# A fused attention, mixture and MLP kernel: MLP weights written to scratch as two parts, and adjoining turns summed in one set of banks

## The chip, the cores and the metric

The kernel runs on one core of a Trainium2 chip. The time is device microseconds for one execution. Before the change three runs gave 1144.51, 1145.59 and 1153.5 us; the median is 1145.59 us.

## What is computed

Three layers follow one another on 1152 tokens of 512 features. The first is attention, local and coarse; its output is the token matrix x. The other two are these, cut to what the change touches:

```python
def _moe_ref(x, w_gate, w1, w2):
    P = ...                      # 8 rounds of row and column scaling of exp(x @ w_gate)
    for e in range(8):           # w1[e] 512 x 1024, w2[e] 1024 x 512
        out += P[:, e:e + 1] * (np.maximum(x @ w1[e], 0.0) @ w2[e])
    return out

def _moe2_ref(x, w_in, w_out):   # w_in 512 x 2048, w_out 2048 x 512
    h = x @ w_in
    g = np.maximum(h, 0.0) + np.log1p(np.exp(-np.abs(h)))
    return g @ w_out
```

w_in and w_out arrive as 64-bit floats; the kernel makes 32-bit floats of them on the chip.

## The kernel before

**Two parts of every operand.** A matmul here takes 32-bit operands in a rounded form. Every operand is therefore split in two: `hi`, the value cast to the rounded form, and `lo`, the value minus `hi`. Three matmuls (hi by hi, hi by lo, lo by hi) make one product.

**Turns.** The MLP is treated as two more experts (`e` = 8 and 9) beside the eight of the mixture. The tokens are in two sets: `s` = 0 with four tiles of 128 tokens (256 columns in each half) and `s` = 1 with five (320 columns in each half). The hidden units of an expert are in four pieces `p`, and `g` is a pair of pieces. A turn is one (e, g, s, p), 80 in all, in the list `steps`. `first(n)` makes the hidden units of a turn by seven products of a fast 2x2 scheme (line 578, banks `m`), so that w1 is kept as OPS = 7 blocks, the first four of them sums. Between the products ACT copies (`t1`, `t5`, `u2`, line 587) and DVE adds (`c`, line 592). `hidden` then applies the activation: for the mixture one ACT and one DVE instruction (lines 539 and 540), for the MLP nine on ACT, DVE and POOL in a chain (lines 545 to 556). `second(n)` multiplies by w2 into banks `yps` (line 637), one for each token tile.

**Banks and sums.** Before the change two turns (`p` even and `p` odd) are summed in the banks. Then `weigh` (lines 648 to 656) reads each bank: into `acc` by a copy the first time, by a plain add for experts 0, 8 and 9 (line 650), and with the gate's weight for experts 1 to 7 (line 654).

**Order of the turns.** Experts 1 to 6 take the sets in the order 0, 1, 0, 1. Experts 0 (its second half), 7, 8 and 9 take them so that several turns of one set follow one another:

```python
late = [(0, 1), (1, 1), (1, 0), (0, 0)]
turn = {E - 1: late, E: late, NE - 1: [(0, 0), (0, 1), (1, 1), (1, 0)]}
```

**Weights.** `fetch_first` and `fetch_second` load the weights of a piece into a place of three (`wp`, three buffers each of w1h, w1l, w2h, w2l). They are called when PE's last use of the place three fetches ago has been issued. For the mixture the raw weights come to a `raw` tile (two buffers), ACT casts hi, POOL and DVE subtract. For the MLP the same is done from scratch in HBM: w1 by two loads of 448 KB (line 117), two casts (line 118), and for each a subtraction on POOL of 512 columns and one on DVE of 384 (line 120); w2 by one load (line 147), two casts (line 151) and two subtractions on POOL (line 152). The MLP does ten such fetches of w1 and ten of w2.

**Conversion.** From turn 12 to turn 58, `convert` (lines 159 to 199) makes 32 pieces of MLP weights, two in three turns: it loads 64-bit values into a `raw` tile, makes 32-bit floats in `cva` with seven DVE instructions (lines 177 to 187), and for w_in (the first 16 pieces) also the four sums on POOL (line 106). It writes `s_in` in three stores and `s_out` in one. `cva` and `sums` share two buffers (`smp`) with the sums that `fetch_first` makes for the mixture.

**What sets the order.** PE's instructions stand in the order written. Those of DVE, ACT, POOL and SP are put in order by a scheduler when the kernel is built, and each engine then runs its own list in that order, waiting where it must. All DMAs are issued by SP.

## Time and profile before

| what | value |
|---|---|
| median of three runs | 1145.59 us |
| the profiled execution's own time | 1142.73 us |
| its span, first to last instruction | 1140.6 us |
| mean granted TensorE clock | 0.981 of full speed |
| PE busy | 1069.6 us (94%) |
| DVE busy | 818.9 us (72%) |
| ACT busy | 532.2 us (47%) |
| POOL busy | 497.6 us (44%) |
| moved by DMA | 93.74 MB, mean 82 GB/s |

Attention fills about the first 150 us, with the first turns of expert 0 beside it. Experts 1 to 7 follow, and the MLP runs from about 910 us to the end. PE is the engine with the most work. A reader looks for the stretches in which it stands idle, and for the engine that ended each idle time.

### The profile page before, as it was taken

Reading aid. Unit: us, or ns where it says so; the run is one execution under the profiler, and the core shown is the slowest. Engines: PE = TensorE matmul, PEld = TensorE weight load, DVE = VectorE, ACT = ScalarE, POOL = GpSimd, SP = SyncE. Lnnn points to the kernel's source line nnn. Section 1 sums busy time; section 2 is a strip of 40 time slices with the busy share of each in tenths; the row PEclk is TensorE's granted clock in tenths of the full one; section 3 lists DMA queues with packets and bytes.
Section 4 is the critical chain, followed back from the end, with each engine's and each line's share of the span. In section 5 each row is a group of like instructions: output and inputs, shape, how many; then the busy total and the mean of one; then the engine's idle time right before and its main releaser. Section 6 shows DMA issues by size and latency. Waiting matters only on the chain.

```text
span 1140.6 us, 17866 instructions
## 1 busy us (share of the span) xinstructions
PE 1069.6 (94%) x6385; PEld 936.7 (82%) x6385; DVE 818.9 (72%) x1680; ACT 532.2 (47%) x1403; POOL 497.6 (44%) x529
## 2 busy tenths in 40 slices
PE   6799998999999999999999999999999879989998
PEld 5678877888988888888988889888888767877887
DVE  6999756754757677676767666677665788888885
ACT  4677644433324334233333334334423577776773
POOL 6744325373344434443542523424532555465331
PEclk9689999999999999999999999999999989999999
DMA  8554101211232332333222322223231332132002
GB/s 172 127 111 109 50 1 56 72 41 38 91 106 75 122 96 83 97 100 107 72 91 93 111 93 66 83 93 93 87 107 62 102 102 70 33 90 77 25 1 83
DMA packets 107736, 93.74 MB, mean 82 GB/s; under 512 B 34560, under 2 KB 86016, under 8 KB 107648
## 3 DMA queue, kind: packets, MB, share of 16 engines
q1 hardware_dynamic: 107648, 92.61, 27.5%
q8 instruction: 50, 0.82, 0.3%
q14 instruction: 38, 0.31, 0.1%
HBM read 78.69 MB, written 13.89 MB: 81 GB/s over the span
## 4 chain that ended last, share of the span: by engine, by line
PE 49%; DVE 29%; DMA 6%; POOL 5%; ACT 5%; issue 5%; SPq 1%; DVEq 0%; POOLq 0%; ACTq 0%
PE yps L637 22%; PE m L578 22%; DVE c L592 3%; DMA raw<-in_moe_w_in 2%; DVE acc L654 2%; DMA raw<-in_moe_w_out 2%; DVE cva L177 2%; DVE cva L178 2%; DVE xl L224 2%; POOL w1l L141 2%; POOL sums L106 2%; DVE raw L184 1%; DVE cva L181 1%; POOL w2l L152 1%; PE sc L349 1%
## 5 line engine op out<-in xcount | busy, mean ns | idle before, releaser
L578 PE MATMUL m<-xh,w1h 128*128 128x320 f32 (+1 forms) x1120 | 339.7, 303 | 43.0 <-DVE c L592 24.8
L578 PE MATMUL m<-xl,w1h 128*128 128x320 f32 (+1 forms) x1120 | 332.8, 297 | 0.0
L578 PE MATMUL m<-xh,w1l 128*128 128x320 f32 (+1 forms) x1120 | 332.7, 297 | 0.0
L578 PEld LDWEIGHTS m<-xh,w1h 128*128 128x128 f32 x1120 | 212.6, 190 | 76.6 <-DVE c L592 40.8
L578 PEld LDWEIGHTS m<-xl,w1h 128*128 128x128 f32 x1120 | 212.8, 190 | 11.5 <-DVE xl L224 0.3
L578 PEld LDWEIGHTS m<-xh,w1l 128*128 128x128 f32 x1120 | 212.7, 190 | 0.0
L637 PE MATMUL yps<-w2h,hh 128*128 128x512 f32 x520 | 207.5, 399 | 1.7 <-ACT hh L555 1.4
L637 PE MATMUL yps<-w2l,hh 128*128 128x512 f32 x520 | 206.4, 397 | 0.0
L152 POOL TENSOR_TENSOR w2l<-raw,w2h 128x512 fp32r<-128x512 f32 x92 | 125.5, 1384 | 182.6 <-ACT w2h L151 182.5
L637 PE MATMUL yps<-w2h,hl 128*128 128x512 f32 x520 | 204.4, 393 | 0.4 <-DVE hl L556 0.4
L539 ACT ACTIVATE hh<-c 128x256 fp32r<-128x256 f32 (+1 forms) x138 | 60.6, 444 | 213.6 <-DVE c L592 213.6
L141 POOL TENSOR_TENSOR w1l<-sums,w1h 128x512 fp32r<-128x512 f32 x72 | 94.9, 1335 | 131.0 <-ACT w1h L140 93.2
L637 PE MATMUL yps<-w2h,h 128*128 128x512 f32 x400 | 140.7, 392 | 0.0
L654 DVE SCALAR_TENSOR_TENSOR acc<-yps,pr,acc 128x512 f32<-128x512 f32 x126 | 93.7, 744 | 50.4 <-PE yps L637 47.7
L637 PEld LDWEIGHTS yps<-w2h,hl 128*128 128x128 f32 x520 | 98.5, 189 | 23.9 <-DVE hl L556 0.8
L592 DVE TENSOR_TENSOR c<-m,t 128x256 f32<-128x256 f32 (+1 forms) x160 | 72.1, 451 | 58.3 <-PE m L578 57.6
L637 PEld LDWEIGHTS yps<-w2h,hh 128*128 128x128 f32 x520 | 99.1, 191 | 15.8 <-ACT hh L555 1.8
L637 PEld LDWEIGHTS yps<-w2l,hh 128*128 128x128 f32 x520 | 99.1, 191 | 11.7
L540 DVE SCALAR_TENSOR_TENSOR hl<-c,hh 128x256 fp32r<-128x256 f32 (+1 forms) x138 | 74.4, 541 | 33.4 <-ACT hh L539 31.2
L552 POOL TENSOR_TENSOR ab<-ab,up 128x320 f32<-128x320 f32 (+1 forms) x64 | 55.3, 865 | 90.1 <-ACT ln L548 43.1
L637 PEld LDWEIGHTS yps<-w2h,h 128*128 128x128 f32 x400 | 75.4, 188 | 13.4
L106 POOL TENSOR_TENSOR sums<-raw 128x256 f32<-128x256 f32 x72 | 62.1, 883 | 50.0 <-DMA raw<-in_moe_w 38.9
(135 smaller groups left out, 1681.3 us busy)
## 6 DMA issues: line engine op xcount, KB each, us to landing
raw<-in_moe_w SPq DMA_DIRECT2D x72, 256.0 KB
raw<-in_moe_w SPq DMA_DIRECT2D x36, 512.0 KB
raw<-s_in SPq DMA_DIRECT2D x20, 448.0 KB
raw<-in_moe_w_in SPq DMA_DIRECT2D x32, 256.0 KB
raw<-in_moe_w_out SPq DMA_DIRECT2D x16, 512.0 KB
raw<-s_out SPq DMA_DIRECT2D x10, 512.0 KB
s_in<-sums SPq DMA_DIRECT2D x16, 256.0 KB
s_out<-cva SPq DMA_DIRECT2D x16, 256.0 KB
```

Of the source, the lines that this page charges most:

```text
L106: nc.gpsimd.tensor_tensor(sums[i], a, b, op=op)
L141: nc.gpsimd.tensor_tensor(lo[:, part], sums, hi[:, part].bitcast(F32), op=ALU.subtract)
L152: nc.gpsimd.tensor_tensor(lo[:, i], raw[:, i], hi[:, i].bitcast(F32), op=ALU.subtract)
L177: nc.vector.tensor_scalar(a, high, 0x07FFFFFF, 3, op0=ALU.bitwise_and, op1=ALU.logical_shift_left)
L178: nc.vector.scalar_tensor_tensor(out=a, in0=low, scalar=29, in1=a, op0=ALU.logical_shift_right, op1=ALU.bitwise_or)
L539: nc.scalar.activation(hh, c, AF.Relu)
L540: nc.vector.scalar_tensor_tensor(out=hl, in0=c, scalar=0.0, in1=hh.bitcast(F32), op0=ALU.max, op1=ALU.subtract)
L552: nc.gpsimd.tensor_tensor(ab, ab, up, op=ALU.subtract)
L578: nc.tensor.matmul(b[:, :h], x[:, i, kk, :], y[s][:, i, kk, :], start=(not more and n == 0), stop=(n == 5), skip_group_check=more,)
L592: nc.vector.tensor_tensor(c, b[:, :h], t, op=ALU.add)
L637: nc.tensor.matmul(y, a[:, f, tok], b[:, f, :], start=(start and m == 0), stop=(stop and m == 5))
L654: nc.vector.scalar_tensor_tensor(out=acc[t], in0=y, scalar=pr[:, t, e : e + 1], in1=acc[t], op0=ALU.mult, op1=ALU.add,)
```

## The change

Scratch now holds both parts of every MLP weight, in the layout of the operand places. `convert` makes them: after the conversion ACT casts hi into the `raw` tile, whose values are no longer needed, and POOL subtracts in place. That is two casts and two subtractions of 128x512 for each w_in piece and one of each for a w_out piece, 48 and 48 in all. A w_in piece is then written by six stores instead of three, in runs of 512 bytes, and a w_out piece by two instead of one. For the MLP `fetch_first` and `fetch_second` only issue two loads each, straight into hi and lo; 896 KB each for w1 and 512 KB each for w2. The casts and subtractions that they had (20 casts of 896 columns, 20 of 512, 40 subtractions on POOL, 20 on DVE) are gone.

A list `begins` marks the turns at which a new sum starts in the banks: where the set changes, or the expert (8 and 9 counting as one), and at the first five. Turns that follow one another in the same set and expert are summed in the same banks. `weigh` is called at the end of a sum, 32 instructions fewer: five plain adds in expert 0, nine weighted ones in expert 7, eighteen plain adds in the MLP.

```diff
-    s_in = scratch("s_in", [F2 // (2 * P), 2, P, OPS, P])
-    s_out = scratch("s_out", [F2, DM])
+    s_in = scratch("s_in", [F2 // (2 * P), 2, P, OPS, 2, P])
+    s_out = scratch("s_out", [F2 // (2 * P), 2, P, 2, DM])
...
         if e >= E:
-            for kk in range(2):
-                raw = rawp.tile([P, OPS, P], F32, tag="raw", name="raw7")
-                nc.sync.dma_start(raw, s_in[n - E * NP, kk])
-                nc.scalar.copy(hi[:, :, kk], raw)
-                for engine, part in zip((nc.gpsimd, nc.vector), parts):
-                    engine.tensor_tensor(
-                        lo[:, part, kk], raw[:, part], hi[:, part, kk].bitcast(F32), op=ALU.subtract
-                    )
+            for i, x in enumerate((hi, lo)):
+                nc.sync.dma_start(x.bitcast(F32), s_in[n - E * NP, i])
             return
...
     def fetch_second(f, n):
...
+        if e >= E:
+            for i, x in enumerate((hi, lo)):
+                nc.sync.dma_start(x.bitcast(F32), s_out[n - E * NP, i])
+            return
...
     def convert(i):
...
+        def parts(x, hi, engine):
+
+            nc.scalar.copy(hi, x)
+            engine.tensor_tensor(x.bitcast(F32R), x, hi.bitcast(F32), op=ALU.subtract)
+
+
+        first = raw.rearrange("p d f c -> p (d f c)").bitcast(F32R)
         if i >= HALVES:
-            nc.sync.dma_start(s_out[rows, :], a)
+            e, h, p = (i - HALVES) // (2 * NP), (i - HALVES) // NP % 2, (i - HALVES) % NP
+            first = first[:, :DM]
+            parts(a, first, nc.gpsimd)
+            for j, x in enumerate((first.bitcast(F32), a)):
+                nc.sync.dma_start(s_out[e * NP + p, j, :, h], x)
             return
         a = a.rearrange("p (q c) -> p q c", q=4)
+        first = first.rearrange("p (q c) -> p q c", c=P)
         sums = smp.tile([P, SUMS, P], F32, tag="sums", name="sums")
         weight_sums([sums[:, i] for i in range(SUMS)], lambda fh, d: a[:, 2 * d + fh])
-        nc.sync.dma_start(s_in[m, kk, :, :SUMS], sums)
-        nc.sync.dma_start(s_in[m, kk, :, SUMS], a[:, 0])
-        nc.sync.dma_start(s_in[m, kk, :, SUMS + 1 :], a[:, 2:4])
+        parts(sums, first[:, :SUMS], nc.gpsimd)
+        parts(a, first[:, SUMS:], nc.gpsimd)
+        for j, x, y in ((0, *[first.bitcast(F32)[:, part] for part in (slice(SUMS), slice(SUMS, 2 * SUMS))]), (1, sums, a)):
+            nc.sync.dma_start(s_in[m, j, :, :SUMS, kk], x)
+            nc.sync.dma_start(s_in[m, j, :, SUMS, kk], y[:, 0])
+            nc.sync.dma_start(s_in[m, j, :, SUMS + 1 :, kk], y[:, 2:4])
...
+    begins = [
+        n == 0 or s != steps[n - 1][2] or min(e, E) != min(steps[n - 1][0], E) or n < BESIDE + 1
+        for n, (e, g, s, p) in enumerate(steps)
+    ]
+    stops = begins[1:] + [True]
...
     def weigh(e, s, i, y):
-        t = TILES[s][i]
+        t, e = TILES[s][i], min(e, E)
...
-        elif e == 0 or e >= E:
+        elif e in (0, E):
...
-                second(n, *hs, i, ys[i], p % 2 == 0, p % 2 == 1)
-                if p % 2:
+                second(n, *hs, i, ys[i], begins[n], stops[n])
+                if stops[n]:
                     weigh(e, s, i, ys[i])
```

PE's list is the same instruction for instruction; the other four lists move. Three places follow, a pair of pieces of before and after each.

ACT's list in the MLP, where the hidden units of turn 72 are begun (`t` and `u` are the copies out of the banks, `ab`, `ln` and `h` belong to the activation, `w2h` to the weights). Before:

```order
1002 L587 COPY t_10935<-m_10928 128x256
1003 L587 COPY t_10944<-m_10937 128x256
1004 L151 CAST w2h<-raw_10914 128x512 x2
1005 L545 ACTIVATE ab<-c_10959 128x256
1006 L555 CAST h_10761<-ab 128x256 x2
1007 L546 ACTIVATE ab<-ab 128x256
1008 L548 ACTIVATE ln<-ab 128x256
1009 L587 COPY u_10979<-m_10928 128x256
```

And in the changed kernel:

```order
1024 L605 COPY t_10945<-m_10938 128x256
1025 L573 CAST h_10795<-ab 128x256
1026 L605 COPY t_10954<-m_10947 128x256
1027 L573 CAST h_10795<-ab 128x256
1028 L563 ACTIVATE ab<-c_10969 128x256
1029 L564 ACTIVATE ab<-ab 128x256
1030 L566 ACTIVATE ln<-ab 128x256
1031 L605 COPY u_10989<-m_10938 128x256
```

The two casts of w2h, which waited for a load from scratch, no longer stand ahead of `u`.

DVE's list at the second piece of w_in that is converted (`cva` and the 64-bit `raw` are the conversion, `c` and `hl` the hidden units). Before:

```order
530 L540 SCALAR_TENSOR_TENSOR h_3529<-m_3530,h_3528 128x320
531 L654 SCALAR_TENSOR_TENSOR acc<-yps,pr,acc 128x512
532 L177 TENSOR_SCALAR cva<-raw_3642 128x512
533 L592 TENSOR_TENSOR c_3699<-m_3692,t_3675 128x256
534 L178 SCALAR_TENSOR_TENSOR cva<-raw_3642,cva 128x512
535 L181 SCALAR_TENSOR_TENSOR cva<-raw_3642,cva 128x512
```

And in the changed kernel:

```order
526 L558 SCALAR_TENSOR_TENSOR h_3526<-m_3527,h_3525 128x320
527 L610 TENSOR_TENSOR c_3703<-m_3696,t_3679 128x256
528 L558 SCALAR_TENSOR_TENSOR hl<-c_3703,hh 128x256
529 L173 TENSOR_SCALAR cva<-raw_3639 128x512
530 L174 SCALAR_TENSOR_TENSOR cva<-raw_3639,cva 128x512
531 L610 TENSOR_TENSOR c_3727<-m_3681,u_3713 128x256
```

The start of the conversion (line 177 before, 173 now) has moved behind the first `c` and `hl` of the next turn.

SP's list at a w_in piece in the middle of the conversion (`raw<-in_moe_w_in` loads the next piece's 64-bit values, `raw<-in_moe_w` weights of the mixture). Before:

```order
97 L198 DMA s_in<-cva 128x128
98 L199 DMA s_in<-cva 128x256
99 L126 DMA raw_4502<-in_moe_w 128x4x128 x2
100 L126 DMA raw_4616<-in_moe_w 128x4x128 x2
101 L197 DMA s_in<-sums 128x512
102 L168 DMA raw_4633<-in_moe_w_in 128x2x256 x2
```

And in the changed kernel:

```order
111 L210 DMA s_in<-raw_4411 128x128
112 L211 DMA s_in<-raw_4411 128x2x128
113 L209 DMA s_in<-raw_4411 128x4x128
114 L210 DMA s_in<-cva 128x128
115 L211 DMA s_in<-cva 128x2x128
116 L209 DMA s_in<-sums 128x4x128
117 L119 DMA raw_4648<-in_moe_w 128x4x128 x2
118 L164 DMA raw_4665<-in_moe_w_in 128x2x256 x2
```

Six stores now stand together, the last three behind POOL's subtractions, and the next loads stand behind all six.

## Rows read from the trace of the kernel before

**Rows 1.** The page: span, then busy time of each engine.

```profile
span 1140.6 us, 17866 instructions
...
PE 1069.6 (94%) x6385; PEld 936.7 (82%) x6385; DVE 818.9 (72%) x1680; ACT 532.2 (47%) x1403; POOL 497.6 (44%) x529
```

**Rows 2.** Stretches: length, PE, PEld, DVE, ACT, POOL busy; clock, DMA share, GB/s.

```profile
270.00:600.00 330.00, 319.67 (x1851) 284.44 (x1849) 226.26 (x392) 114.59 (x268) 143.99 (x172) 1.00 0.30 92
600.00:850.00 250.00, 244.83 (x1396) 217.05 (x1397) 168.65 (x306) 89.93 (x207) 92.88 (x86) 1.00 0.28 91
...
870.00:1075.00 205.00, 180.11 (x1027) 156.34 (x1026) 170.29 (x333) 144.11 (x350) 104.14 (x88) 0.97 0.23 72
```

**Rows 3.** All waits of PE from 270 to 850 us: total, times, longest.

```profile
PE m L578 <- DVE c L592: 15.5, 22, 1.6
```

**Rows 4.** Longest waits of PE from 870 to 1075 us.

```profile
PE m L578 <- ACT u L587: 11.9, 8, 4.7
PE m L578 <- DVE c L592: 8.3, 10, 2.0
PE tp L664 <- ACT xf L667: 1.5, 2, 0.7
```

**Rows 5.** Groups by line, 870 to 1075 us: busy, mean ns, idle before, releasers.

```profile
L120 POOL TENSOR_TENSOR w1l<-raw,w1h 128x512 fp32r<-128x512 f32 x20 | 32.2, 1630 | 27.1 <-ACT w1h L118 27.0
L152 POOL TENSOR_TENSOR w2l<-raw,w2h 128x512 fp32r<-128x512 f32 x20 | 29.8, 1512 | 16.6 <-ACT w2h L151 16.5
L120 DVE TENSOR_TENSOR w1l<-raw,w1h 128x384 fp32r<-128x384 f32 x20 | 19.7, 990 | 4.0 <-ACT w1h L118 4.0
L118 ACT CAST w1h<-raw 128x896 fp32r<-128x896 f32 x20 | 18.0, 942 | 2.3 <-PE m L578 1.4 <-DMA raw<-s_in 0.6
L151 ACT CAST w2h<-raw 128x512 fp32r<-128x512 f32 x20 | 11.4, 617 | 9.4 <-DMA raw<-s_out 8.6 <-PE yps L637 0.4 <-DMA raw<-in_moe_w 0.4
L650 DVE TENSOR_TENSOR acc<-yps,acc 128x512 f32<-128x512 f32 x12 | 8.2, 680 | 0.5 <-PE yps L637 0.5
...
L654 DVE SCALAR_TENSOR_TENSOR acc<-yps,pr,acc 128x512 f32<-128x512 f32 x9 | 6.7, 741 | 1.2 <-PE yps L637 1.2
```

**Rows 6.** Timeline, ACT and PE around two waits: start, length, instruction, idle before.

```profile
929.37 1.15 ACT L151 CAST w2h<-raw 128x512 fp32r<-128x512 f32 x2
936.06 0.64 PE L578 MATMUL m<-xh,w1h 128*128 128x320 f32 x1 [4.74 <-ACT u L587]
1028.19 1.15 ACT L151 CAST w2h<-raw 128x512 fp32r<-128x512 f32 x2 [1.18 <-DMA raw<-s_out]
1031.68 0.35 ACT L587 COPY u<-m 128x256 f32<-128x256 f32 x1
1032.09 0.39 PE L578 MATMUL m<-xh,w1h 128*128 128x256 f32 x1 [2.17 <-ACT u L587]
```

**Rows 7.** One stretch around the longer wait of rows 6, columns as in rows 2.

```profile
926.00:944.00 18.00, 12.35 (x59) 10.73 (x59) 16.77 (x29) 15.14 (x39) 12.01 (x11) 0.72 0.24 81
```

**Rows 8.** Waits of SP's queue over the whole span.

```profile
SPq L117 <- POOL w2l L152: 56.6, 9, 11.3
...
SPq L117 <- DVE w1l L120: 32.6, 5, 18.4
```

**Rows 9.** Groups by line and shape, 270 to 850 us.

```profile
L177 DVE TENSOR_SCALAR cva<-raw 128x512 uint32<-128x512 uint32 x31 | 27.3, 882 | 29.3 <-DMA raw<-in_moe_w_out 11.2 <-DMA raw<-in_moe_w_in 9.9 <-POOL w1l L141 5.6
...
L140 ACT CAST w1h<-sums 128x512 fp32r<-128x512 f32 x48 | 29.5, 615 | 19.7 <-POOL sums L106 19.7
...
L141 POOL TENSOR_TENSOR w1l<-sums,w1h 128x512 fp32r<-128x512 f32 x48 | 63.7, 1344 | 73.2 <-ACT w1h L140 52.5 <-PE yps L637 20.7
```

**Rows 10.** Line 177 over the whole span: ns shortest/median/longest.

```profile
L177 DVE TENSOR_SCALAR cva<-raw x32: 426/430/1506, 295.3 to 856.1; 128x512 uint32<-128x512 uint32 x32
```

**Rows 11.** Timeline, POOL and DVE at one start of a conversion.

```profile
343.81 2.55 POOL L141 TENSOR_TENSOR w1l<-sums,w1h 128x512 fp32r<-128x512 f32 x2 [1.85 <-ACT w1h L140]
345.15 1.50 DVE L177 TENSOR_SCALAR cva<-raw 128x512 uint32<-128x512 uint32 x1 [0.55 <-POOL w1l L141]
```

More of the change, by code (lines that the diff above doesn't have):

```diff
@@ L112, in fetch_first @@
         weights.setdefault(f, {})[0] = hi, lo
-        parts = slice(0, SUMS), slice(SUMS, OPS)
         if e >= E:
-            for kk in range(2):
-                raw = rawp.tile([P, OPS, P], F32, tag="raw", name="raw7")
-                nc.sync.dma_start(raw, s_in[n - E * NP, kk])
-                nc.scalar.copy(hi[:, :, kk], raw)
-                for engine, part in zip((nc.gpsimd, nc.vector), parts):
-                    engine.tensor_tensor(
-                        lo[:, part, kk], raw[:, part], hi[:, part, kk].bitcast(F32), op=ALU.subtract
-                    )
+            for i, x in enumerate((hi, lo)):
+                nc.sync.dma_start(x.bitcast(F32), s_in[n - E * NP, i])
             return
@@ L144, in fetch_second @@
         e, p = divmod(n, NP)
-        w = w2[e] if e < E else s_out[(e - E) * FF : (e - E + 1) * FF, :]
-        raw = rawp.tile([P, 2, DM], F32, tag="raw", name="raw2")
-        nc.sync.dma_start(raw, w.rearrange("(h a p) d -> p h a d", h=2, p=P)[:, :, p, :])
         hi = wp.tile([P, 2, DM], F32R, tag="w2h", name="w2h")
         lo = wp.tile([P, 2, DM], F32R, tag="w2l", name="w2l")
+        weights.setdefault(f, {})[1] = hi, lo
+        if e >= E:
+            for i, x in enumerate((hi, lo)):
+                nc.sync.dma_start(x.bitcast(F32), s_out[n - E * NP, i])
+            return
+        raw = rawp.tile([P, 2, DM], F32, tag="raw", name="raw2")
+        nc.sync.dma_start(raw, w2[e].rearrange("(h a p) d -> p h a d", h=2, p=P)[:, :, p, :])
         for i in range(2):
@@ L152, in fetch_second @@
             nc.gpsimd.tensor_tensor(lo[:, i], raw[:, i], hi[:, i].bitcast(F32), op=ALU.subtract)
-        weights.setdefault(f, {})[1] = hi, lo
     TINY = 2.0 ** -15 * 1.125
@@ L765, in attention_moe_mlp @@
             e, g, s, p = steps[n]
-            if p % 2 == 0:
+            if begins[n]:
                 ys = outputs(s)
```

## The prediction

> **What bounds the kernel now.** I read the page first, then the busy time by stretches, then PE's waits in two of the stretches, then what the change removes and adds there, and last the timeline at single waits. PE is busy for 1069.6 of 1140.6 us [rows 1], so PE bounds the kernel, and a change that leaves its list as it is can win only from the idle time and from TensorE's clock. Where that time lies is shown by the stretches [rows 2]. From 270 to 850 us (experts 1 to 7, with the conversion beside them) PE stands idle for 330 - 319.7 + 250 - 244.8 = 15.5 us, under 3%. From 870 to 1075 us (the last turns of expert 7 and most of the MLP) it stands idle for 205 - 180.1 = 24.9 us, 12%. DVE is busy for 170.3 of these 205 us (83%, against 67% from 600 to 850 us) and ACT for 144.1 (70%, against 36%). PE's waits in the MLP stretch are for ACT's copy `u` (11.9 us) and DVE's add `c` (8.3 us), both of which give PE a bank back [rows 4]; no wait for weights is among its longest. So in the MLP two crowded engines hand the banks back late.
>
> The timeline shows how [rows 6]. At 1028.19 us ACT stood for 1.18 us before a cast of w2h, until the load from scratch had landed, and cast for 1.15 us; the copy `u` came at 1031.68, and PE, which had waited 2.17 us for it, went on at 1032.09. The longest wait, 4.74 us, ended at 936.06 and has a cast of w2h of 1.15 us on ACT before it as well. Around it the granted clock is 0.72 over 18 us [rows 7], where it is 1.00 in the stretches without such a wait [rows 2]: part of the time it stood at the lower level, 1.2 GHz.
>
> **The change part by part.** *What the MLP loses.* From 870 to 1075 us these go [rows 5]: on ACT 18.0 us (line 118) and 11.4 (line 151), on POOL 32.2 and 29.8, on DVE 19.7 (line 120) and, by the longer sums, 12 plain adds of 8.2 us and 4 of the weighted ones, 4 x 0.741 = 3.0 us. DVE goes to 170.3 - 30.9 = 139.4 us (68%), ACT to 114.7 (56%), POOL from 104.1 to 42.1 (21%). DVE is then as busy as from 600 to 850 us (168.65 of 250, 67%), and there PE is idle for 5.17 of 250 us; over 205 us that is 4.2 us. Two things stay: the transposes' waits for `xf`, 1.5 us [rows 4], and part of the 4.74 us wait, since between 929 and 936 us the cast of w2h is one ACT instruction among copies and casts of the tokens that stay. I keep half of it, 2.4 us. So 4.2 + 1.5 + 2.4 = 8.1 us idle are left of 24.9: a gain of 16.8 us. It is bounded by 24.9 and by 6, half of the waits for `u` alone.
>
> *The clock.* Over those 18 us [rows 7] PE was busy for 12.35 us on 59 matmuls. At the rate of 600 to 850 us (1396 in 244.83 us busy, 5.70 per us) they take 10.35 us. I count the 2.0 us as gained, since the drop stands with the waits; the bounds are 0 and 3.5, as a shorter drop lies in the rest of the stretch (0.97 over all).
>
> *The longer sums outside that stretch.* Five plain adds in expert 0 and five weighted ones in expert 7 go: 5 x 0.68 + 5 x 0.74 = 7.1 us of DVE. From 270 to 850 us PE waited 15.5 us, all for `c` [rows 3], beside 394.9 us of DVE work, 0.04 us for each; so 0.3 us, between 0 and 7.1. The banks themselves are no term: no wait of matmuls into `yps` for a reader of the banks is among the longest [rows 4].
>
> *What the conversion gains in work.* POOL gets 48 subtractions of 128x512, at 1.344 us [rows 9] 64.5 us, on top of 144.0 + 92.9 = 236.9 us. ACT gets 48 casts at 0.615 us, 29.5 us, on 204.5. DVE gets nothing, but its instructions stretch where POOL works beside them: line 177 takes 0.426 us at best [rows 10], 0.882 on average [rows 9], and 1.50 us beside two subtractions of POOL [rows 11]. If PE's 15.5 us of waits grow as POOL's work does, 15.5 x 64.5 / 236.9 = 4.2 us are added. ACT's new casts of sums wait for POOL as line 140's do (19.7 us over 48, so 0.41 us each). PE had no wait for ACT in this stretch [rows 3], so I put them at 1 us. Together 5.2 us. No row shows a conversion with these parts, so the bounds are wide: nothing, and 30 us if the 29.3 us that DVE stands before line 177 today [rows 9] doubles and PE sees it all.
>
> *A rule that speaks against this part.* The Trainium skill (SBUF — State Buffer, "SBUF: two separate sides") says that DVE and GpSimd share a pair of ports as an exclusive lock: whoever starts first holds it for its whole instruction and the other blocks. Rows 11 agree, as line 177 takes 1.50 us beside POOL's. By that rule every added subtraction could hold DVE up for all of its 1.34 us, and the result would be the third rival below.
>
> *Loads and stores.* The MLP loads twice as much: 2 x 896 + 2 x 512 = 2816 KB a fetch. DMA moves 72 GB/s at a share of 0.23 [rows 2], 313 GB/s at full share, so 9.2 us a fetch. A fetch is issued when PE has left the place three fetches back. Today the loads stand waiting at SP for a raw tile (56.6 us for POOL's line 152, 32.6 for DVE's line 120 [rows 8]), pass through ACT, POOL and DVE, and still no wait of PE for weights is among the longest. Without these steps twice the bytes cost nothing; if that cover is gone, see the fourth rival. In the conversion, SP's list holds the next loads behind all six stores, which wait for POOL. For the mixture's weights I take the cost as nothing, by the same reserve; for the next piece it makes line 173 late, which is in the bound of 30 us.
>
> *Sum.* The profiled execution took 1142.73 us (span 1140.6 and 2.1 around it): 1142.7 - 16.8 - 2.0 - 0.3 + 5.2 = 1128.8, so 1129 us. It lies 2.9 us under the median of the runs shown, which differ among themselves by 9; I don't carry this over.
>
> **The rivals.**
> - *All of it, at no price.* Only the transposes' 1.5 us stay, and the conversion hides its work in ACT's and POOL's idle time (65% and 59% of 270 to 850 us [rows 2]). 1142.7 - 23.4 - 2.0 - 0.3 = 1117 us. Against it: DVE at 68% has never run without waits of PE.
> - *PE waits for a chain, not for crowded engines.* The MLP's activation is nine instructions in a row on three engines, and that remains. Then only half of the waits for `u` goes: 1142.7 - 6 + 5.2 = 1142 us. For it: no earlier stretch has this chain. Against it: the casts stand in ACT's list directly ahead of `u`.
> - *DVE and POOL block each other in the conversion.* The 48 subtractions put 64.5 us on DVE, which is idle for 580 - 394.9 = 185 us there. If PE sees a third of it, 21.5 us, the result is 1142.7 - 19.1 + 21.5 + 1 = 1146 us: no change. Against it: line 177's average excess is 0.46 us, not 1.34.
> - *The loads come late.* The first four turns of expert 8 need a fetch each. If each kept PE waiting for half a load, 4 x 4.6 = 18.4 us would eat the gain: 1142.7 - 19.1 + 5.2 + 18.4 = 1147 us.
> - *Slower: the conversion holds DVE at its first instruction.* A w_in piece keeps its raw tile, `cva` and `sums` until the second part's store has landed, longer by two casts, two subtractions (3.9 us) and a landing. Line 177 waits for raw tile and `cva` already (29.3 us [rows 9], up to 3 us at once), and `c` for PE stands behind it in DVE's list. If each of 16 w_in pieces costs PE 2 us and each of 16 w_out pieces 1 us, that is 48 us: 1142.7 - 19.1 + 48 = 1172 us. It decides from 19.1 / 32 = 0.6 us a piece. Against it: the scheduler has moved line 173 back in DVE's list.
>
> **How the numbers follow.** One per cent, 11.5 us, is about what a measurement of this kernel tells from no change: faster means under 1134.1 us, slower over 1157. My forecast has 0.57, the first rival 0.13; both are faster: 0.70. The chain has 0.12, the blocking 0.07, the late loads 0.04: within 1%, 0.23. The last rival has 0.07: slower. The range runs from 1113, a little under the first rival (whose 1117 keeps a clock term of 2 where 3.5 is the bound), to 1143, which takes in the chain; beyond it lie the other three, 0.18 together.
>
> **What would show it.** Right: from 870 us on, DVE near 68% and POOL near 21% busy, PE's waits for `u` down to 2 or 3 us, the stretch some 17 us shorter, and no drop of the clock to 1.2 GHz that lasts 10 us; from 270 to 850 us the same work in about 5 us more, with PE's waits for `c` near 20 us. Wrong in the MLP: PE waits for `hh`, `hl` or `c` as long as before though ACT and DVE are idle (the chain), or for a DMA into w1h or w2h (the loads). Wrong in the conversion: the idle time before line 173 far over 29.3 us, with PE's waits for `c` growing by as much.

## The result and the profile after

The changed kernel takes 1137.88 us (median of 10 runs, 1133.66 to 1142.66) where the kernel before takes 1149.80 us beside it (10 runs, 1144.51 to 1153.50): a ratio of 0.990, with a 95% interval of 0.987 to 0.993. It is faster, by 11.9 us. Forecast was 1129 us from a profiled execution of 1142.73, so 13.7 us less. The prediction set its mark for faster, 1134.1 us, one per cent under the early median of 1145.59; one per cent under 1149.80 is 1138.3, and the measured time lies just below that.

The page of the changed kernel gives the span and the busy times, beside [rows 1]:

```profile
span 1140.9 us, 18021 instructions
...
PE 1077.5 (94%) x6385; PEld 943.2 (83%) x6385; DVE 781.3 (68%) x1628; ACT 536.3 (47%) x1411; POOL 498.8 (44%) x537
```

The two profiled spans are alike, 1140.6 and 1140.9 us, though the medians lie 11.9 us apart. PE runs the same 6385 matmuls in the same order in both, so two of them can serve as marks: the last product of the gates, which ends the attention, and the first transposition of `acc`, behind expert 7. The rows of the two tiles give first and last start behind the shortest/median/longest ns. First the kernel before:

```profile
L462 PE MATMUL lt<-xl,wgs x16: 276/298/317, 140.8 to 157.0; 128*16 128x256 f32 x8, 128*16 128x320 f32 x8
...
L664 PE MATMUL tp<-ident,acc x36: 270/272/329, 873.3 to 931.1; 128*128 128x128 f32 x36
```

Then the changed kernel:

```profile
L474 PE MATMUL lt<-xl,wgs x16: 276/298/317, 149.5 to 165.9; 128*16 128x256 f32 x8, 128*16 128x320 f32 x8
...
L682 PE MATMUL tp<-ident,acc x36: 270/272/329, 896.1 to 948.3; 128*128 128x128 f32 x36
```

So the attention took 157.0 us before and 165.9 after, the experts with the conversion 873.3 - 157.0 = 716.3 and 896.1 - 165.9 = 730.2, and the MLP to the end of the span 267.3 and 244.8: +8.9, +13.9 and -22.5. The program of the attention is the same in both. What differs there is above all the granted clock in the first 100 us, as the stretches of the two show (columns as in [rows 2]), first before, then after:

```profile
0.00:100.00 100.00, 80.06 (x600) 65.91 (x601) 85.70 (x259) 64.15 (x255) 58.96 (x85) 0.86 0.59 129
```

```profile
0.00:100.00 100.00, 77.91 (x530) 63.54 (x530) 77.71 (x235) 57.70 (x230) 50.90 (x80) 0.73 0.55 123
```

Over the thirteen kernels of this study with just this attention (all but e12_free, which moves a tile of it) it took 156.4 to 165.9 us: the +8.9 is chance of one execution. The other two stages give -8.6 us, inside the interval of the medians (-8.0 to -14.6).

PE's idle time and its busy time have both changed in these two stages, as the stretches between the marks show (columns as in [rows 2]). First the kernel before, the conversion and then the MLP:

```profile
157.00:873.30 716.30, 696.54 (x4000) 618.54 (x3998) 474.69 (x880) 254.29 (x590) 295.31 (x315) 1.00 0.27 85
873.30:1140.60 267.30, 238.51 (x1345) 207.66 (x1343) 214.14 (x428) 177.53 (x432) 119.97 (x107) 0.97 0.20 62
```

Then the changed kernel:

```profile
165.90:896.10 730.20, 703.60 (x3999) 622.08 (x3998) 491.17 (x870) 281.50 (x638) 362.45 (x363) 0.99 0.32 99
896.10:1140.90 244.80, 233.46 (x1345) 205.83 (x1343) 159.12 (x386) 154.12 (x392) 57.38 (x67) 0.98 0.34 128
```

In the MLP PE is idle for 11.3 us instead of 28.8 and busy 5.0 us less. In the conversion it is idle for 26.6 us instead of 19.8, and busy 7.1 us more for the same matmuls, at a granted clock of 0.99 instead of 1.00. An estimate from the clock: 0.98 from 157 to 270 us is 2.3 us of full speed lost before; 0.97 from 165.9 to 270 us and the two drops shown in the last section are 6.5 us after. So some 4 of the 7.1 us go with the clock; the rest is not explained.

The stretches of the changed kernel, where [rows 2] has those of before:

```profile
270.00:600.00 330.00, 317.70 (x1822) 280.64 (x1821) 225.05 (x379) 128.87 (x292) 181.74 (x197) 0.99 0.37 110
600.00:850.00 250.00, 241.23 (x1369) 213.33 (x1368) 177.45 (x298) 96.07 (x218) 112.53 (x102) 0.99 0.31 102
870.00:1075.00 205.00, 196.55 (x1142) 172.89 (x1141) 133.99 (x320) 127.08 (x324) 52.72 (x58) 0.98 0.40 149
```

From 870 us on PE is idle for 205 - 196.6 = 8.5 us (24.9 before) and issues 1142 matmuls in that time instead of 1027. DVE is down to 65%, ACT to 62%, POOL to 26%, and the DMA engines move twice as much. PE's waits there, beside [rows 4]:

```profile
PE m L596 <- DVE c L610: 4.6, 8, 1.4
PE m L596 <- ACT u L605: 2.2, 1, 2.2
PE tp L682 <- ACT xf L685: 1.5, 2, 0.7
```

The waits for `u` have gone from 11.9 us to a single one of 2.2, and no load is among the waits. From 270 to 850 us PE waits more than in [rows 3]:

```profile
PE m L596 <- DVE c L610: 16.5, 18, 2.3
PE m L596 <- DVE h L558: 2.4, 4, 0.8
PE m L596 <- ACT u L605: 1.6, 4, 0.6
PE m L596 <- DVE hl L558: 0.4, 1, 0.4
```

That is 20.9 us against 15.5, in a stretch of fixed ends; over the same matmuls the middle stage is the larger +13.9, of which the 7.1 us of busy time are no wait at all.

How PE comes to wait beside a conversion is seen on the timeline. At 538 us DVE, ACT and PE of the changed kernel, in order of time:

```profile
537.57 0.42 DVE L610 TENSOR_TENSOR c<-m,t 128x256 f32<-128x256 f32 x1
537.73 0.62 ACT L190 CAST raw<-cva 128x512 fp32r<-128x512 f32 x1 [2.73 <-DVE cva L183]
538.26 0.41 ACT L557 ACTIVATE h<-c 128x256 fp32r<-128x256 f32 x1
538.71 0.68 DVE L558 SCALAR_TENSOR_TENSOR h<-c,h 128x256 fp32r<-128x256 f32 x1 [0.72 <-ACT h L557]
...
539.74 0.62 ACT L190 CAST raw<-sums 128x512 fp32r<-128x512 f32 x1 [1.06 <-POOL sums L106]
539.97 0.41 DVE L610 TENSOR_TENSOR c<-m,u 128x256 f32<-128x256 f32 x1
540.41 0.42 ACT L557 ACTIVATE h<-c 128x256 fp32r<-128x256 f32 x1
540.86 0.48 DVE L558 SCALAR_TENSOR_TENSOR h<-c,h 128x256 fp32r<-128x256 f32 x1 [0.48 <-ACT h L557]
541.26 0.74 DVE L672 SCALAR_TENSOR_TENSOR acc<-yps,pr,acc 128x512 f32<-128x512 f32 x1
541.92 0.41 DVE L610 TENSOR_TENSOR c<-m,t 128x256 f32<-128x256 f32 x1
...
542.38 0.39 PE L596 MATMUL m<-xh,w1h 128*128 128x256 f32 x1 [2.26 <-DVE c L610]
```

The first cast delays the tokens a little: the last `c` before it, of 537.57, has ended at 537.99, and `h` begins at 538.26, behind the cast of `cva`. The second cast stands 1.06 us for POOL, but costs `h` nothing here, since the `h` of 540.41 begins as the `c` of 539.97 ends, at 540.38. The `c` that PE waits 2.26 us for, at 541.92, stands in DVE's list behind an `h` that waits 0.48 us for ACT and behind an `acc` of 0.74. So at this place the casts explain only a few tenths of a microsecond of PE's wait.

### The profile page after: what moved, and what is told of

It is laid out like the page before. It is cut to its first block, busy times and chain, and to the rows that moved or that the text cites. A ratio compares the mean times of both kernels' runs of the same rounds, so it can differ in the third digit from the quotient of the medians.

```text
span 1140.9 us, 18021 instructions
## 1 busy us (share of the span) xinstructions
PE 1077.5 (94%) x6385; PEld 943.2 (83%) x6385; DVE 781.3 (68%) x1628; ACT 536.3 (47%) x1411; POOL 498.8 (44%) x537
## 4 chain that ended last, share of the span: by engine, by line
PE 57%; DVE 21%; DMA 7%; POOL 6%; issue 5%; ACT 3%; SPq 1%; DVEq 0%; POOLq 0%; ACTq 0%
PE yps L655 26%; PE m L596 25%; DMA raw<-in_moe_w_out 2%; POOL sums L106 2%; DMA raw<-in_moe_w_in 2%; DVE c L610 2%; DVE acc L672 2%; DVE cva L173 2%; PE sc L361 1%; DVE xl L236 1%; DVE cva L174 1%; POOL w1l L134 1%; DVE raw L180 1%; DVE cva L177 1%; DVE cva L181 1%
## 5 line engine op out<-in xcount | busy, mean ns | idle before, releaser
L149 POOL TENSOR_TENSOR w2l<-raw,w2h 128x512 fp32r<-128x512 f32 x72 | 97.3, 1370 | 125.1 <-ACT w2h L148 125.1
L672 DVE SCALAR_TENSOR_TENSOR acc<-yps,pr,acc 128x512 f32<-128x512 f32 x117 | 87.1, 744 | 45.8 <-PE yps L655 43.0
L655 PEld LDWEIGHTS yps<-w2h,hh 128*128 128x128 f32 x520 | 99.0, 190 | 14.1 <-DVE acc L668 0.6
L558 DVE SCALAR_TENSOR_TENSOR hl<-c,hh 128x256 fp32r<-128x256 f32 (+1 forms) x138 | 85.1, 620 | 35.0 <-ACT hh L557 33.7
L605 ACT COPY t<-m 128x256 f32<-128x256 f32 (+1 forms) x160 | 62.5, 397 | 40.9 <-PE m L596 39.4
```

The source lines that it names most:

```text
L149: nc.gpsimd.tensor_tensor(lo[:, i], raw[:, i], hi[:, i].bitcast(F32), op=ALU.subtract)
L558: nc.vector.scalar_tensor_tensor(out=hl, in0=c, scalar=0.0, in1=hh.bitcast(F32), op0=ALU.max, op1=ALU.subtract)
L605: nc.scalar.copy(t, b[:, :h])
L655: nc.tensor.matmul(y, a[:, f, tok], b[:, f, :], start=(start and m == 0), stop=(stop and m == 5))
L672: nc.vector.scalar_tensor_tensor(out=acc[t], in0=y, scalar=pr[:, t, e : e + 1], in1=acc[t], op0=ALU.mult, op1=ALU.add,)
```

## The experiments

The marks above give for every kernel the length of the three stages. The table has each beside its measured ratio; "conversion" is the stage from the last product of the gates to the first transposition of `acc`, "MLP" from there to the end of the span.

| kernel | conversion, us | PE idle in it | PE busy in it | MLP, us | ratio to before (95%) |
|---|---|---|---|---|---|
| before | 716.3 | 19.8 | 696.5 | 267.3 | 1 |
| changed | 730.2 | 26.6 | 703.6 | 244.8 | 0.990 (0.987 to 0.993) |
| e0_same | 731.5 | 28.0 | 703.5 | 244.1 | 0.988 (0.984 to 0.992) |
| e1_direct | 730.6 | 30.3 | 700.3 | 245.9 | 0.992 (0.989 to 0.995) |
| e2_sums | 713.9 | 19.5 | 694.4 | 263.0 | 0.993 (0.990 to 0.996) |
| e3_nosub | 726.5 | 28.0 | 698.5 | 245.1 | 0.988 (0.984 to 0.993) |
| e4_stores | 717.2 | 20.8 | 696.5 | 244.6 | 0.980 (0.978 to 0.982) |
| e9_hold | 723.0 | 24.2 | 698.8 | 244.4 | 0.981 (0.977 to 0.985) |
| e10_casts | 724.0 | 24.6 | 699.4 | 244.6 | 0.981 (0.977 to 0.985) |
| e11_pool | 736.2 | 34.8 | 701.4 | 245.3 | 0.994 (0.991 to 0.997) |
| e12_free | 728.3 | 25.9 | 702.4 | 244.1 | 0.990 (0.987 to 0.994) |
| e6_act | 732.9 | 29.2 | 703.7 | 257.4 | 1.002 (1.000 to 1.004) |
| e8_dve | 732.4 | 29.0 | 703.4 | 250.0 | 0.996 (0.994 to 0.999) |
| e5_first | 843.6 | 122.7 | 720.9 | 245.1 | 1.086 (1.083 to 1.089) |

Up to the end of the conversion the changed kernel, e0_same, e6_act and e8_dve are one program. Its four executions took 730.2 to 732.9 us, mean 731.8: differences of under 3 us between two single profiles show nothing. Every other edit also moves the scheduler's lists, even where the work is the same: DVE's list in e9_hold leaves that of e4_stores at its 631st instruction. A difference between two such kernels is that of the part together with its new order, and no run here separates the two.

**e0_same: the changed kernel again.**

> The changed kernel once more, to see what differs between two executions of one program. Theory: the work is the same, so PE's waits from turn 8 on come out within 1 us of the first profile (about 31 us in all), and only TensorE's clock differs, above all in the attention, whose program is that of the kernel before. The ratio to before stays at 0.990 within 0.003. Rival: the waits themselves scatter by 5 us or more, and single profiles can't be compared by their waits.

1135.14 us (6 runs), ratio 0.988. The stages repeat: +15.2 us in the conversion and -23.2 in the MLP. PE's waits from 270 us to the end are 31.7 us against 30.1, a little over the 1 us expected and far from the rival's 5.

**e1_direct: the two-part weights, with sums every two turns.**

```diff
-    begins = [
-        n == 0 or s != steps[n - 1][2] or min(e, E) != min(steps[n - 1][0], E) or n < BESIDE + 1
-        for n, (e, g, s, p) in enumerate(steps)
-    ]
+    begins = [p % 2 == 0 for e, g, s, p in steps]
```

> The first part of the change alone: weights in two parts, loaded straight into their places, but every two turns summed as before. Theory: nearly all of the gain in the MLP is from this part; PE's waits after 858 us are within 3 us of the changed kernel's, the ratio to before is about 0.992. Rival: the longer sums, which take 32 DVE instructions away, carry half of the gain; then the ratio is 0.995 or more and 8 to 10 us of waits come back.

1140.74 us (12 runs), ratio 0.992. The MLP is 21.4 us shorter than before, so nearly the whole gain there comes with the direct loads; their price in the conversion, 14.3 us here, comes with them.

**e2_sums: the kernel before, with the longer sums alone.**

> The second part of the change alone: the longer sums, with the weights as before. Theory: 18 of the 32 DVE instructions that go are in the MLP, 12 us of DVE; PE's waits there fall by 2 to 4 of 28 us and the ratio to before is 0.997 to 1.0. Rival: the sums carry half of the gain, 0.995. No cost in the conversion is expected by either.

1140.24 us (12 runs), ratio 0.993: more than the theory gave, and more than the rival's 0.995. The profile shows 267.3 - 263.0 = 4.3 us in the MLP and 2.4 us in the stage before it. With the direct loads in place the sums bring only 245.9 - 244.8 = 1.1 us of the MLP (1.8 against e0_same), under what single profiles can show: both parts relieve DVE, and what one has given the other can't give again. In time the sums alone have 9.6 us and the direct loads alone 9.1, against 14.7 for the whole change in this comparison: the sums cost the conversion nothing, and most of what the direct loads gain in the MLP is spent there.

**e3_nosub: the conversion without its subtractions on POOL.**

```diff
             nc.scalar.copy(hi, x)
-            engine.tensor_tensor(x.bitcast(F32R), x, hi.bitcast(F32), op=ALU.subtract)
```

> The changed kernel without the subtractions in the conversion: the second part is stored as the whole value, so the outputs are not the reference's. 48 POOL instructions go, 64 us of POOL. Theory of the prediction (POOL stretches and delays DVE): PE's waits between 270 and 850 us fall from 21 us back to 15 or 16 us, as before the change. Rival (ACT's new casts stand in its list and wait for POOL's sums): they stay near 20 us. Gain in time by the theory some 5 us, by the rival 1 us.

1135.01 us (4 runs), ratio 0.988; e0_same has 1135.14 us in the same comparison, so in time no gain is seen, though four runs do not rule out one of 5 us. The conversion takes 726.5 us, 5.3 under the mean of the changed kernel's program, but still 10.2 more than before. PE's waits from 270 to 850 us did not fall: they are 23.0 us, where the theory expected 15 or 16 and the rival about 20. PE's idle time in the conversion is 28.0 us, as with the subtractions (26.6 to 29.2); the 5.3 us lie in its busy time, 698.5 us against 703.4 to 703.7. DVE did get faster without them:

```profile
161.80:888.30 726.50, 698.46 (x4000) 619.81 (x3998) 465.42 (x870) 280.24 (x638) 297.84 (x315) 1.00 0.32 99
```

Its 870 instructions take 465.4 us instead of 491.2, for 64.6 us less of POOL's work, and PE's idle time does not show it. SP's waits from 270 to 858 us have six groups like these two, 56.3 us together, which the kernel before has not at all:

```profile
SPq L164 <- DMA s_in<-raw: 19.9, 8, 3.5
SPq L146 <- DMA s_out<-raw: 10.8, 6, 2.3
```

The next loads into raw wait for stores out of raw to land, since the first part now lies there. Theory A of the next runs was formed on this. But in the changed kernel, with its subtractions, such waits come to 3.5 us in all: there other waits of SP end last.

**e4_stores: neither casts nor subtractions, only the doubled stores.**

```diff
         def parts(x, hi, engine):

-            nc.scalar.copy(hi, x)
-            engine.tensor_tensor(x.bitcast(F32R), x, hi.bitcast(F32), op=ALU.subtract)
+            return
...
-            for j, x in enumerate((first.bitcast(F32), a)):
+            for j, x in enumerate((a, a)):
...
-        for j, x, y in ((0, *[first.bitcast(F32)[:, part] for part in (slice(SUMS), slice(SUMS, 2 * SUMS))]), (1, sums, a)):
+        for j, x, y in ((0, sums, a), (1, sums, a)):
```

> The changed kernel without the casts and subtractions of the conversion: it stores the whole value in both places, so the MLP's second parts are not rounded remainders, and that part of the computation is wrong. raw is free early here, as in the kernel before; the stores are as many and as large as in the changed kernel. Theory A (raw held) and rival B (casts and subtractions) both expect PE's waits from 270 to 850 at the 13 to 17 us of the kernel before and a time of 0.980 to 0.984; rival C (the doubled stores, in SP's order or on the DMA engines) expects 19 us or more and 0.987 to 0.990.

1124.74 us (5 runs), ratio 0.980. The conversion takes 717.2 us, 0.9 more than before and 3.3 more than in e2_sums. PE's waits from 270 to 850 us are 17.0 us. Rival C falls: twice the stores and bytes cost little. What the casts, the subtractions and the place of the first part cost together is 731.8 - 717.2 = 14.6 us by the profiles: 7.4 us of idle time and 7.1 of busy time, with the means of the four executions (28.2 and 703.6). In time, 0.980 against 0.988 to 0.990, it is some 9 to 12 us.

**e5_first: the first parts in a tile of pairp.**

```diff
-        first = raw.rearrange("p d f c -> p (d f c)").bitcast(F32R)
+        first = pairp.tile([P, 2, 2 * HALF[1]], F32, tag="pair", name="first")
+        first = first.rearrange("p a c -> p (a c)")[:, : 2 * SUMS * P].bitcast(F32R)
```

> The changed kernel, but the conversion writes its first parts into a tile of the pool pairp, which lies idle there, and not into raw. Theory A (the conversion is dear because raw, of which there are two, is now held until the store of the first part has landed, so that the next loads are issued late and VectorE stands at L173): PE's waits from 270 to 850 fall from 20.9 us to 12 to 16, and the time is 0.981 to 0.985 of the kernel before. Rival B (the casts and subtractions themselves, in the order of ScalarE and GpSimd): the waits stay at 19 to 23 us and the time at 0.987 to 0.990.

1247.11 us (6 runs), ratio 1.086. The expectation rested on a mistake: pairp does not lie idle, since every third turn takes its `hh` and `hl` from it. DVE's group for `h` from 270 to 858 us names what it stood for:

```profile
L559 DVE SCALAR_TENSOR_TENSOR h<-c,h 128x320 fp32r<-128x320 f32 (+1 forms) x38 | 18.0, 524 | 51.3 <-DMA s_in<-first 43.2 <-DMA s_out<-first 7.9
```

The run says nothing on raw. It shows what it costs when a tile on PE's path waits for a store to land: 843.6 - 731.8 = 112 us, with waits of PE of up to 14.0 us for that `h`.

**e9_hold and e10_casts: raw held without casts, and casts without raw held.** e9_hold is e4_stores with the two stores of the first part reading raw. e10_casts is e3_nosub with all stores reading `sums` and `a`.

> As e4_stores (no casts and no subtractions in the conversion, so the computation is changed there in the same way), but the stores of the first part read raw, as in the changed kernel, with whatever bits lie in it, so raw is held until they have landed. Theory A (raw held makes the conversion dear): PE waits some 8 us more from 270 to 850 than in e4_stores, and the time is 0.985 to 0.988 of the kernel before. Rival B (the casts in ScalarE's order): the waits and the time of e4_stores, 0.978 to 0.982.

> The changed kernel with the casts of the conversion into raw, but with no subtraction, and all its stores read the whole value (so the MLP's second parts are whole values, and wrong): raw is free as soon as the cast has ended. Theory A (raw held until its stores have landed): waits and time near e4_stores, 0.978 to 0.983. Rival B (the casts stand in ScalarE's order and wait there for VectorE's last operation and GpSimd's sums): PE's waits from 270 to 850 some 8 us above those of e4_stores, and 0.985 to 0.988.

1129.08 us (6 runs) and 1127.11 us (6 runs), both at a ratio of 0.981. PE's waits from 270 to 850 us are 20.5 and 20.9 us, 3.5 and 3.9 more than in e4_stores, where each theory expected some 8 of its own part. By the profiles raw held costs 723.0 - 717.2 = 5.8 us, the casts 724.0 - 717.2 = 6.8 us; both together (e3_nosub) 9.3 us. In PE's idle time alone it is 3.4, 3.8 and 7.2 us. So neither theory has it alone. The times put the two nearer to e4_stores than the profiles do (0.981 against 0.980, with intervals of 0.004 to either side).

**e11_pool: the casts on GpSimd.**

```diff
-            nc.scalar.copy(hi, x)
+            engine.tensor_copy(hi, x)
```

> The changed kernel with the casts of the conversion on GpSimd instead of ScalarE, where the sums are made already and where the profile shows room (181.74 us busy of the 330 from 270 to 600); nothing is left out. If rival B holds (ScalarE standing at casts), PE's waits from 270 to 850 fall by 4 to 8 us and the time to 0.981 to 0.985 of the kernel before, below the changed kernel. If theory A holds (raw held), they stay or rise, since raw is held for some microseconds more: 0.988 to 0.995.

1143.80 us (12 runs), ratio 0.994, above the changed kernel's 0.990 though the intervals touch, and the conversion takes 736.2 us, 3.3 more than the longest of the four executions. The time is in theory A's range, but not for its reason. PE has a wait from 270 to 850 us that no other kernel shows:

```profile
PE m L596 <- DVE c L610: 18.8, 17, 2.5
PE m L596 <- ACT w1h L133: 6.1, 2, 4.5
PE m L596 <- POOL w1l L134: 2.4, 3, 1.0
```

POOL makes the sums of the mixture's weights too; with the casts in its list these come late, ACT's `w1h` behind them, and PE waits for a weight.

**e12_free: the first parts in a tile of their own.**

```diff
-    tmpp = ctx.enter_context(tc.tile_pool(name="tmpp", bufs=11))
+    tmpp = ctx.enter_context(tc.tile_pool(name="tmpp", bufs=10))
...
-        first = raw.rearrange("p d f c -> p (d f c)").bitcast(F32R)
+        first = cvp[0].tile([P, 2 * SUMS * P], F32R, tag="first", name="first")
...
-    rest = const.tile([P, KD, LEFT], F32, name="rest")
+    rest = ap.tile([P, KD, LEFT], F32, bufs=1, name="rest")
```

> The changed kernel, whole, but the first parts of the conversion are written into a tile of their own (4 KB a partition, one of it) instead of raw, so raw is free at VectorE's last read of it; for the room, tmpp has 10 tiles instead of 11 and rest lies in the attention's pool. If the price of the conversion is raw's hold and the casts in about equal parts, as the two runs before show, PE's waits from 270 to 850 fall from 20.9 us to 15 to 18 and the time to 0.983 to 0.987 of the kernel before. Rival (the lost tile of tmpp makes t, u or c late): the waits from 870 to 1075 rise above 12 us, and the time is 0.990 or more.

1132.99 us (12 runs, 1128.89 to 1145.28), ratio 0.990, as the changed kernel's. The conversion takes 728.3 us, 3.5 under the mean of 731.8 and 1.9 under the shortest of the four. PE's waits from 270 to 850 us did not fall, against the expectation:

```profile
PE m L598 <- DVE c L612: 15.0, 16, 2.3
PE m L598 <- DVE h L560: 5.5, 5, 3.2
```

With two small groups, of 0.8 and 0.6, they are 21.9 us. What DVE stood for before the conversion's first instruction from 270 to 858 us (total, times) suggests why:

```profile
  POOL w1l L134: 11.7, 9
  DMA s_in<-cva: 10.4, 6
  DMA raw<-in_moe_w_out: 8.7, 7
  DMA raw<-in_moe_w_in: 2.2, 2
```

In the changed kernel, from 270 to 850 us, it was this:

```profile
L173 DVE TENSOR_SCALAR cva<-raw 128x512 uint32<-128x512 uint32 x29 | 27.6, 953 | 32.4 <-POOL w1l L134 11.6 <-DMA raw<-in_moe_w_out 10.4 <-DMA raw<-in_moe_w_in 6.2
```

The waits for loads have shrunk from 16.6 us to 10.9, and one of 10.4 us for the stores out of `cva` to land has taken their place: the next piece needs both tiles, and the later one binds. That the one wait has kept PE's waits up in place of the other is argued, not shown. The rival falls too, though the time is at its 0.990: the MLP took 244.1 us.

**e6_act: ScalarE's casts of the MLP put back, into a tile that nobody reads.**

```diff
+            for kk in range(2):
+                idle = rawp.tile([P, 2 * SUMS, P], F32R, tag="raw", name="idle")
+                old = [weights[f - 1][0][i][:, :, kk].bitcast(F32) for i in range(2)]
+                nc.scalar.copy(idle[:, :OPS], old[0])
...
+            for i in range(2):
+                nc.scalar.copy(idle[:, i], old[0][:, i])
```

> The changed kernel, with the ScalarE casts of the MLP's weights put back (as many and as large as in the kernel before), but of a weight part that is already there into a tile that nobody reads: work without a load to wait for. Theory (PE waited for u because ScalarE stood behind casts whose loads were late): the gain stays, PE's waits from 870 to 1075 at 8 to 12 us, the time at 0.987 to 0.992. Rival (ScalarE's busy time itself): waits of 16 us or more, the time at 0.995 or above.

1150.40 us (12 runs), ratio 1.002: the whole gain is gone, as the rival had it. The MLP takes 257.4 us, 12.6 more than in the changed kernel; the 9.9 us that it still is shorter than before are eaten by the conversion. PE's waits from 870 to 1075 us:

```profile
PE m L604 <- ACT u L613: 13.1, 7, 5.1
PE m L604 <- DVE c L618: 2.5, 4, 1.1
PE tp L690 <- ACT xf L693: 1.5, 2, 0.7
```

The wait for `u` is back, at 13.1 us (11.9 before), and the three groups have 17.1 us, in the rival's range. So it is the casts in ACT's list that made `u` late. The run was to tell ACT's work from its standing before loads, and can't, whatever its numbers: the added casts read the weights of the fetch before, and those were not always there.

```profile
L119 ACT CAST idle<-w1h 128x896 fp32r<-128x896 f32 x20 | 18.1, 939 | 7.1 <-DMA w1h<-s_in 7.1
...
L151 ACT CAST idle<-w2h 128x512 fp32r<-128x512 f32 x20 | 11.6, 620 | 7.0 <-DMA w2h<-s_out 7.0
```

29.7 us of work and 14.1 us of standing came back together. Which of them weighs more stays open.

**e8_dve: twenty subtractions of 384 columns on VectorE in the MLP.**

> The changed kernel, with twenty VectorE subtractions of 384 columns put back in the MLP, of parts that are there into a tile that nobody reads. Theory (VectorE's share makes c late): PE's waits for c from 870 to 1075 rise from 4.6 us to 7 to 10, the time by 2 to 5 us to 0.990 to 0.993. Rival (VectorE had room; only the loads mattered): no change, 0.987 to 0.990.

1145.14 us (12 runs), ratio 0.996, more than the 0.990 to 0.993 expected. The MLP takes 5.2 us more than in the changed kernel. PE's waits for `c` have doubled, from 4.6 us, and the added work stood for loads as well:

```profile
PE m L600 <- DVE c L614: 9.6, 11, 2.9
```

```profile
L119 DVE TENSOR_TENSOR idle<-w1h,w1l 128x384 fp32r<-128x384 f32 x20 | 13.3, 704 | 7.2 <-DMA w1l<-s_in 7.2
```

DVE was the second engine that the change relieved, and this part of its work, put back, takes about 5 us of the 22.5. POOL's removed work was not put back by itself.

## Why the prediction was right, and where its terms were off

Sign and size held: 1137.88 us measured lies in the range, and 11.9 us were gained where 13.7 were forecast. But two terms were off, in opposite directions, and that the sum came so near is in part luck: by the profiles the MLP gave 22.5 us where 18.8 were forecast, and the conversion took 13.9 where 4.9 were (5.2, less 0.3 for the sums).

*What the MLP loses: right.* Forecast were 16.8 us less idle time; over the same matmuls PE's idle time fell by 17.5, from 28.8 to 11.3 us. The idle time left from 870 to 1075 us is 8.5 us (forecast 8.1), with DVE at 65% (68), one wait for `u` of 2.2 us (2.4 kept) and `xf` at 1.5. That stretch holds 26 us of expert 7 in the changed kernel, so the stage between the marks is the better comparison. The step from "the engine is as crowded as in the experts" to "PE waits as it does there" gave the right number. POOL is at 26%, not 21, as parts of the conversion fall into the stretch.

*The clock: right in kind, too small.* It was put at 2.0 us, with a bound of 3.5; PE's busy time in the MLP fell by 5.0 us for the same matmuls. In [rows 7] the clock of 0.72 over 18 us means 18 x 0.28 / 0.5 = 10 us at 1.2 GHz. What is left stands around the remaining wait for `u`, of 2.17 us:

```profile
944.00:962.00 18.00, 14.42 (x72) 12.44 (x71) 15.10 (x40) 14.37 (x40) 4.51 (x5) 0.81 0.60 229
```

By the same working that is 18 x 0.19 / 0.5 = 6.8 us. Before, there is a second drop, 0.88 from 1026 to 1040 us, around the wait of 2.17 us in [rows 6], 14 x 0.12 / 0.5 = 3.4 us more, which the prediction had in its bound alone. So the time at 1.2 GHz falls from about 13.4 to 6.8 us, an estimate of 3.3 us of full speed gained. The remaining 1.7 us of busy time are not explained.

*The longer sums: under-sized in one sense.* Put at 0.3 us outside the MLP, they brought 2.4 there in e2_sums (inside what single profiles scatter by) and 0.7% in time by themselves. In the MLP their share was counted within DVE's relief, which is where it belongs: together with the direct loads they add 1 to 2 us of the MLP.

*What the conversion gains in work: the step that failed.* It was put at 5.2 us, 4.2 for POOL's subtractions and 1 for ACT's casts, all of it waits of PE. Over the same matmuls it is 13.9 to 16.6 us, and three things in it were wrong.

First, the clock in this stage was put at nothing: the sum has a clock term for the MLP alone. Half of the price, 6.9 to 7.1 us, is PE's busy time, with the granted clock at 0.99 instead of 1.00.

Second, the step for the subtractions, that PE's waits grow as POOL's work does, failed. The conversion is 731.8 - 726.5 = 5.3 us shorter without them, near the 4.2 forecast, but that is a coincidence: PE's idle time is 28.0 us without them and 26.6 to 29.2 with them, and the timed runs show no gain (1135.01 us beside 1135.14).

Third, the casts and the held raw were under-sized. The casts were put at 1 us, since PE had no wait for ACT in this stretch. In e10_casts they cost 6.8 us, 3.8 of it idle time of PE, and PE's waits there are for `c`, with 0.8 us for ACT's `u`. In the changed kernel the casts stood longer than the 0.41 us counted, mostly for DVE:

```profile
L190 ACT CAST raw<-cva 128x512 fp32r<-128x512 f32 x29 | 18.0, 620 | 37.2 <-DVE cva L183 32.9 <-DMA raw<-in_moe_w 3.7 <-issue 0.6
...
L190 ACT CAST raw<-sums 128x512 fp32r<-128x512 f32 x16 | 9.9, 621 | 11.8 <-POOL sums L106 11.8
```

That the tokens' `hh` and `h` queue behind them, and PE meets the delay as a later `c`, is argued; the timeline above shows a few tenths of a microsecond of it at one place. Raw held until the first part's stores have landed I had named and put at nothing in the sum; it costs 5.8 us in e9_hold, 3.4 of it idle time. How much of either price is left in the changed kernel, where SP hardly waits for those stores and e12_free frees raw without a gain that shows, stays open, as does the share of the new order of the lists. The bound of 30 us held all this.

*The rivals.* All at no price is out by the conversion. The chain is out: the MLP gained 22.5 us, not 6. For the blocking of DVE and POOL the Trainium skill (SBUF — State Buffer, "SBUF: two separate sides") has the rule that a DVE instruction in a two-port mode or with two inputs in SBUF and a POOL instruction hold the shared ports in turn, each for its whole length. The trace agrees in kind: with the 64.6 us of subtractions DVE's instructions take 25.8 us longer (491.2 against 465.4 in e3_nosub), where being held up by each in full would be 64.5. As a price the rival is out, since PE's idle time is the same with and without them. PE never waited for a load in the MLP. The slower case is out as well: DVE's idle time before line 173 is 32.4 us from 270 to 850, against 29.3 before line 177 [rows 9].

What the prediction had wrong beside this is its basis: the profiled execution of before, 1142.73 us, lies under every one of its ten timed runs in this comparison (1144.51 at least). That shifted the forecast down by 7 us against their median of 1149.80; the difference forecast is what compares.

## What to carry to other kernels

Work that is moved from a crowded stage to a roomier one is not free, even where the engines that take it have room: here a gain of 22.5 us had a price of 14 us. Half of that price was no wait: PE was busy longer with the same matmuls, in part at a lower granted clock. So compare busy time over the same instructions as well as waits. Measure such a move stage by stage between the same two instructions, not over the span: a chance of 9 us in a stage that wasn't touched made two equal spans. And leave out one part at a time: a size that comes out right, as that of the subtractions did, does not show that the reason was right. A tile that becomes the source of a store is held until the store lands; that freeing it helps only if no other tile of the same step is held as long is what e12_free suggests.

## What the runs showed of the hardware

The granted clock of the attention, whose program is the same everywhere, differs from execution to execution: 0.86 and 0.73 in the first 100 us shown above. In the conversion, PE's waits of about 2 us were followed by a drop only at times. After the waits of 1.91 us that ended at 364.00 and of 2.24 us at 643.29 the clock fell for some microseconds; after those of 1.91 us at 515.25 and 2.26 us at 542.38 it stayed at 2.4 GHz:

```profile
358.00:368.00 10.00, 8.09 (x36) 6.75 (x35) 9.86 (x19) 3.86 (x9) 3.31 (x6) 0.83 0.14 41
636.00:650.00 14.00, 11.76 (x58) 10.03 (x57) 8.18 (x17) 3.63 (x8) 2.64 (x3) 0.88 0.13 48
```

```profile
505.00:550.00 45.00, 40.68 (x236) 35.47 (x235) 29.14 (x49) 16.35 (x37) 24.75 (x27) 1.00 0.39 114
```

Before, with no wait over 1.6 us from 270 to 850, the clock is 1.00 throughout [rows 2, 3].

DVE's instructions stretch beside POOL's: the 870 of the conversion took 491.2 us with the 48 subtractions on POOL and 465.4 without, 25.8 us for 64.6 us of POOL's work; the lists stand in another order in the two. PE's idle time was the same, 26.6 to 29.2 us in the four executions with them and 28.0 without.
